# Issuing the first large load ahead of SyncE's part of the entry barrier, in a decode kernel that streams weights and cache

## The chip, the cores and the metric

The kernel runs on one core of one Trainium2 chip. The metric is device microseconds of one execution, in medians of several. The profile's span (first to last instruction) is about 1.25 us shorter than the time of the same run.

## The reference, cut to what matters

One decode step (one token, batch of 2, width 640): adaLN modulation from `c`, attention over the last 1024 positions of a cache with 32 heads of 192, then a gated FFN. At batch 2 nearly all of the work is reading weights and cache once.

```python
x = A_x
mod = (_silu(c) @ w_mod).reshape(c.shape[0], 6, 1, -1)      # w_mod: 640 x 3840
sa, ca, ga, sb, cb, gb = (...)                              # six rows of mod
h = _layernorm(x) * (1 + ca) + sa
x = x + ga * _A_ref(h, A_k_cache, A_v_cache, A_wq, A_wo)    # q = h @ wq, attention, @ wo
h = _layernorm(x) * (1 + cb) + sb
x = x + gb * _B_ref(h, B_w_gate, B_w_up, B_w_down)          # gelu(h@w_gate) * (h@w_up) @ w_down
```

## The kernel before

It moves 77 MB, all large loads by SyncE on one DMA queue, in the order of need: `w_mod`, `wq` (two loads), then K and V tiles through a ring of eight slots, `wo`, and the FFN weights. A small scheduler records every operation with what it reads and writes, works out semaphore waits, and emits one list for each engine at the end. Loads all stand in one line of a helper (L266).

```python
def k_dma(dst, src):
    return lambda e: e.dma_start(dst, src)                   # L266
...
wm_dma = S.dma("sp", k_dma(wm_v..., w_mod...), sem_wm, writes=["wm"], name="ld_wm")
declare_ring()                      # wq (2 loads), K tiles 0 and 1, V tile 0: no wait, the slots are free
S.op("pool", lambda e: e.memset(xr[:, :], 0.0), writes=["xr"], name="xr0")
S.dma("act", k_dma(crow[:, :], c[:, :]), sem_c, writes=["crow"], name="ld_c")
S.dma("act", k_dma(xr[0:P:RB, :], A_x...), sem_x, writes=["xr"], name="ld_x")
... # constants on GpSimd; cT -> SiLU -> scT; x -> statistics; mod = scT @ w_mod -> hT; q = hT @ wq; ...

S.resolve()
S.emit("sp", nc.sync, tail=lambda e: e.wait_ge(sem_out, 16))
S.emit("pool", nc.gpsimd)
S.emit("act", nc.scalar)
S.emit("dve", nc.vector)
S.emit("pe", nc.tensor)
```

Ahead of all of this stands an entry barrier that the program object puts in when it is made (the line of that call, L715, is on its records). GpSimd writes four small constants. Every other engine has a drain (the instruction with which it reports to the barrier) that adds one to a semaphore; GpSimd waits for those four counts, then adds to a second semaphore, and each engine takes its release from that. The barrier keeps any engine from reading the constants before they are written. The load of `w_mod` reads none of them and writes a buffer that nobody has touched yet.

## Time and profile before

| | before |
|---|---|
| time, median (range) of 5 runs | 188.94 us (188.71 to 189.14) |
| span of the profiled run | 187.6 us |
| SyncE's load queue, share of 16 DMA engines' time | 97.1% |
| share of DMA in the chain of waits | 71% |
| first packet of SyncE's queue, from the packet records | 1.81 us |

The page first. The second part cuts the span into 40 slices (the digits are tenths of the slice); the third lists the queues with packets, MB and their share; the fourth is the chain that ended last; the sixth gives KB of one load and the median us from issue to landing.

```profile
DMA  7999998999999999999999999999999999999991
GB/s 254 402 451 435 430 459 372 422 435 424 430 422 422 427 425 426 427 424 420 419 432 432 422 423 422 421 438 422 424 423 422 419 488 428 416 384 442 398 396 45
...
q1 hardware_dynamic: 6492, 76.88, 97.1%
...
DMA 71%; DVE 15%; PE 7%; ACT 2%; SPq 2%; issue 1%
...
ring<-in_A_k_cache_dram SPq DMA_DIRECT2D x16, 1536.0 KB, 24.4
```

The DMA engines have work from the first slice to the last but one. A K tile takes 24.4 us to land, but 1536 KB at about 425 GB/s need only 3.7 us: it waits behind six or seven others. So a K load that is issued a few us sooner or later, because a slot came free sooner or later, should change nothing. Where does a load stream like this leave room? In its start and in what follows its end. These are in the timeline (start us, duration us, engine, line, operation; in brackets, how long the engine had been idle and what ended that) of the first microseconds:

```profile
0.80 0.39 SPq L266 DMA_DIRECT2D r<-in_w_mod_dram  x1
0.81 0.56 ACTq L266 DMA_DIRECT2D crow<-in_c_dram  x1
...
1.25 1.16 SPq L266 DMA_DIRECT2D ring<-in_A_wq_dram  x2
1.30 1.76 DVE L367 MEMSET ps<- 128x2048 f32 x1 [1.30 <-PEq L715]
1.41 0.64 ACTq L266 DMA_DIRECT2D xr<-in_A_x_dram  x1
...
3.43 0.19 ACT L386 ACTIVATE scT<-ps 128x10 bf16<-128x10 bf16 x1
...
9.84 0.24 DVE L388 CAST X<-xr 128x160 f32<-128x160 bf16 x1 [4.33 <-DMA xr<-in_A_x_dram]
...
15.18 2.18 PE L445 MATMUL ps<-r,scT 128*17 128x480 bf16 x20 [3.94 <-DMA r<-in_w_mod_dram]
...
19.58 0.17 DVE L427 CAST hT<-ps 128x10 bf16<-128x10 f32 x1 [0.48 <-PE ps L423]
```

and, from the chain of waits, its second `wq` load, its last K load, the last `w_down` load and the tail:

```profile
1.70 32.29 DMA ring<-in_A_wq_dram
...
120.47 24.62 DMA ring<-in_A_k_cache_dram
...
152.72 31.64 DMA r<-in_B_w_down_dram
...
184.41 0.72 PE ps L684 x16
```

SyncE's own drain and its wait are not in the timeline, which counts work. The records of the trace have them (us from the span's start, duration in ns):

```
0.000    7 SyncE   DRAIN            adds to the first semaphore
0.130   10 VectorE DRAIN            "
0.143    8 ScalarE DRAIN            "
0.316    8 TensorE DRAIN            "
0.304..0.499 GpSimd four constant memsets; its own drain 0.370 to 0.549
0.594   17 GpSimd  waits for four counts
0.672   17 GpSimd  adds to the second semaphore
0.714   17 SyncE   takes its release
0.799  385 SyncE   issues w_mod
1.812      first packet of w_mod
```

SyncE was the first to arrive, at 0.01 us, and then stood for 0.7 us with the whole load stream behind it.

### The profile page before, as it was taken

How to read it: one execution, taken by the hardware profiler on the slowest of the kernel's cores; microseconds unless marked ns; L12 is line 12 of the kernel's file. 1: busy time of each engine (PE TensorE's matmuls, PEld its weight loads, DVE VectorE, ACT ScalarE, POOL GpSimd, SP SyncE). 2: the span in 40 equal slices, each digit the busy share in tenths (PEclk: the TensorE clock that was granted, in tenths of full speed). 3: DMA queues.
4: the chain of work that ended last, by engine and by line, in shares of the span. 5: the costliest groups of instructions: out<-in, count | busy, mean ns of one | idle time of the engine just before them, and what ended most of it. 6: DMA issues, size and time to landing. Idle time of an engine off the chain costs nothing.

```text
span 187.6 us, 2409 instructions
## 1 busy us (share of the span) xinstructions
PE 107.5 (57%) x1039; PEld 51.1 (27%) x1039; DVE 98.2 (52%) x147; ACT 29.9 (16%) x72; POOL 5.1 (3%) x23
## 2 busy tenths in 40 slices
PE   0014730742968887676676655675497395364462
PEld 0011200210323443333423323233253152353121
DVE  6131100019588988886595695775865933003211
ACT  3041100082001221112011110210120103103400
POOL 8200000000000000000000000000000000000000
PEclk9999999997587999999879999999969967569696
DMA  7999998999999999999999999999999999999991
GB/s 254 402 451 435 430 459 372 422 435 424 430 422 422 427 425 426 427 424 420 419 432 432 422 423 422 421 438 422 424 423 422 419 488 428 416 384 442 398 396 45
DMA packets 6518, 77.03 MB, mean 411 GB/s; under 512 B 746, under 2 KB 876, under 8 KB 1516
## 3 DMA queue, kind: packets, MB, share of 16 engines
q1 hardware_dynamic: 6492, 76.88, 97.1%
q8 instruction: 8, 0.13, 0.3%
q10 hardware_dynamic: 16, 0.01, 0.0%
q14 instruction: 2, 0.02, 0.0%
HBM read 76.88 MB, written 0.00 MB: 410 GB/s over the span
## 4 chain that ended last, share of the span: by engine, by line
DMA 71%; DVE 15%; PE 7%; ACT 2%; SPq 2%; issue 1%
DMA ring<-in_A_k_cache_dram 37%; DMA ring<-in_A_wq_dram 17%; DMA r<-in_B_w_down_dram 17%; DVE prod L490 9%; PE ps L502 4%; DVE S_sb L509 4%; PE ps L467 2%; SPq L266 2%; ACT qbc L483 2%; DVE ps L485 1%; DVE M L512 1%; ACT qrow L474 1%; PE ps L526 0%; DVE bcR L519 0%; PE ps L684 0%
## 5 line engine op out<-in xcount | busy, mean ns | idle before, releaser
L490 DVE TENSOR_TENSOR prod<-ring,qbc 128x3072 bf16<-128x3072 bf16 x32 | 55.9, 1751 | 14.3 <-DMA ring<-in_A_k_cache_dram 14.3
L502 PE MATMUL ps<-prod,ident_b 128*128 128x512 bf16 x192 | 52.9, 419 | 14.4 <-DVE prod L490 14.4
L502 PEld LDWEIGHTS ps<-prod,ident_b 128*128 128x128 bf16 x192 | 17.5, 104 | 40.2 <-DVE prod L490 17.5
L509 DVE TENSOR_REDUCE S_sb<-ps 128x32 f32<-128x1024 f32 x16 | 19.3, 1206 | 2.1 <-PE ps L502 2.1
L526 PE MATMUL ps<-bcR,bcL 5*128 5x4 f32 x32 | 6.1, 258 | 21.9 <-DVE bcR L519 21.9
L563 ACT ACTIVATE On<-ps,rden 128x384 bf16<-128x384 f32 x16 | 9.3, 580 | 43.5 <-DVE rden L561 21.1
L551 PE MATMUL ps<-ring,E_sb 128*8 128x384 bf16 x256 | 15.5, 369 | 0.0
L534 ACT ACTIVATE E_sb<-Sb_sb 128x128 bf16<-128x128 f32 x16 | 5.0, 310 | 56.4 <-DVE Sb_sb L531 56.4
L467 PE MATMUL ps<-ring,hT 128*2 128x512 bf16 x60 | 6.7, 626 | 9.8 <-DMA ring<-in_A_wq_dram 8.8
L526 PEld LDWEIGHTS ps<-bcR,bcL 5*128 5x128 f32 x32 | 4.7, 183 | 26.1 <-DVE bcR L519 26.1
L477 DVE CAST qrow<-ps 128x512 bf16<-128x512 f32 x1 | 0.7, 692 | 15.7 <-PE ps L467 15.7
L622 PE MATMUL ps<-ring,oT 128*17 128x160 bf16 x192 | 5.5, 294 | 5.6 <-DMA ring<-in_A_wo_dram 5.6
L531 DVE TENSOR_TENSOR Sb_sb<-S_sb,ps 128x128 f32<-128x128 f32 x16 | 4.6, 287 | 7.6 <-PE ps L526 7.6
L540 PEld LDWEIGHTS ps<-denp,maskc 128*128 128x128 f32 x32 | 7.1, 224 | 3.7 <-ACT E_sb L534 0.9
L641 DVE TENSOR_TENSOR lnt<-ps,modR 128x160 f32<-128x160 f32 x1 | 0.3, 325 | 12.6 <-PE ps L622 12.6
L445 PE MATMUL ps<-r,scT 128*17 128x480 bf16 x40 | 4.3, 597 | 3.9 <-DMA r<-in_w_mod_dram 3.9
L622 PEld LDWEIGHTS ps<-ring,oT 128*17 128x17 bf16 x192 | 4.9, 117 | 6.2 <-DMA ring<-in_A_wo_dram 6.2
L551 PEld LDWEIGHTS ps<-ring,E_sb 128*8 128x8 bf16 x256 | 5.1, 90 | 3.7 <-issue 1.2
L396 PE MATMUL ps<-st,selstat 128*128 128x2 f32 x4 | 0.9, 298 | 8.6 <-ACT sqj L392 8.6
L467 PEld LDWEIGHTS ps<-ring,hT 128*2 128x2 bf16 x60 | 1.7, 114 | 14.7 <-DMA ring<-in_A_wq_dram 9.7
L576 PE MATMUL ps<-On,zsel 128*128 128x96 bf16 x64 | 5.2, 241 | 0.7 <-ACT On L563 0.7
L540 PE MATMUL ps<-denp,maskc 128*128 128x1 f32 x32 | 5.1, 230 | 0.8 <-ACT E_sb L534 0.8
(81 smaller groups left out, 71.2 us busy)
## 6 DMA issues: line engine op xcount, KB each, us to landing
ring<-in_A_k_cache_dram SPq DMA_DIRECT2D x16, 1536.0 KB, 24.4
ring<-in_A_v_cache_dram SPq DMA_DIRECT2D x16, 1536.0 KB, 24.2
r<-in_w_mod_dram SPq DMA_DIRECT2D x1, 4800.0 KB, 14.3
ring<-in_A_wq_dram SPq DMA_DIRECT2D x1, 4608.0 KB, 32.3
ring<-in_A_wo_dram SPq DMA_DIRECT2D x1, 4480.0 KB, 23.4
ring<-in_A_wq_dram SPq DMA_DIRECT2D x1, 3072.0 KB, 21.2
ring<-in_A_wo_dram SPq DMA_DIRECT2D x1, 2720.0 KB, 24.1
r<-in_B_w_gate_dram SPq DMA_DIRECT2D x1, 1920.0 KB, 25.0
```

Source lines behind the costliest of these rows:

```text
L467: last = e.matmul(ps[32 * i:32 * i + B, n, :], lhsT=hT[:, k, :], rhs=wv[:, kk, i, n * QW:(n + 1) * QW], start=(k == 0), stop=(k == KT - 1) ...
L490: S.op("dve", lambda e: e.tensor_tensor(out=prod[:, 2 * (g % 2) + ci, :, :], in0=ring[:, sl, ci * JC * Dh:(ci + 1) * JC * Dh].rearrange("p ...
L502: last = e.matmul(o_ap, lhsT=ident_b[:, :], rhs=prod[:, pz, :, t * GC:(t + 1) * GC], start=(t == 0), stop=(t == NCH - 1))
L509: S.op("dve", lambda e: e.tensor_reduce(out=S_sb[:, z, :], in_=ps[:, 2 * z:2 * z + 2, :].rearrange("p k (j c) -> p (k j) c", c=GC), axis=A ...
L526: S.op("pe", lambda e: e.matmul(ps[:, BK_T, P:P + HQ], lhsT=bcL[:, :], rhs=bcR[:, z, :], start=True, stop=True), reads=[("bcR", z), "bcL"] ...
L531: S.op("dve", lambda e: e.tensor_tensor(out=Sb_sb[:, z, :, :], in0=S_sb[:, z, :].unsqueeze(2).broadcast_to([P, J, HQ]), in1=ps[:, BK_T, P: ...
L534: S.op("act", lambda e: e.activation(out=E_sb[:, z, :, :], in_=Sb_sb[:, z, :, :], func=ACTF.Exp, scale=SCALE, accum_out=denp[:, z:z + 1]), ...
L540: S.op("pe", lambda e: e.matmul(ps[:, BK_T, P + 16:P + 17], lhsT=maskc[:, :], rhs=denp[:, z:z + 1], start=True, stop=True), reads=[("denp" ...
L551: last = e.matmul(ps[32 * i:32 * i + 2 * HQ, BK_O, 0:ON], lhsT=E_sb[:, z, 2 * jp:2 * jp + 2, :].rearrange("p j h -> p (j h)"), rhs=ring[:, ...
L563: S.op("act", lambda e: e.activation(out=On[:, quad % 2, b, :], in_=ps[:, BK_O, 0:ON], func=ACTF.Identity, scale=rden[:, z:z + 1]), reads= ...
L576: last = e.matmul(ps[:, BK_OT, 0:B * NT].rearrange("p (b t) -> p b t", b=B), lhsT=zsel[:, jj, x:x + P], rhs=On[:, quad % 2, :, jj * Dh + d ...
L622: last = e.matmul(ps[32 * i:32 * i + RM, BK_M, 0:DR], lhsT=oT[:, t, :], rhs=wv[:, tl, i, :], start=(t == 0), stop=(t == NT - 1), tile_posi ...
```

## The change: intent and diff

The intent is to start the load stream while the other engines are still coming to the barrier. The instruction that issues `w_mod` is emitted first, cut from the end of the instruction list, and put ahead of SyncE's drain. No other instruction differs.

```diff
         S.resolve()
+        body = nc.main_func.blocks[0].instructions
+        entry = next(i for i, x in enumerate(body) if x.opcode == "Drain" and x.engine == mybir.EngineType.SP)
+        first = S.lists["sp"].pop(0)
+        assert first is wm_dma and not first.waits
+        n0 = len(body)
+        first.fn(nc.sync).then_inc(first.sem, first.inc)
+        moved = body[n0:]
+        del body[n0:]
+        body[entry:entry] = moved
         S.emit("sp", nc.sync, tail=lambda e: e.wait_ge(sem_out, 16))
```

## The prediction

> **What bounds the kernel now.** The load stream. The page's slice rows show the DMA engines 90% or more busy in nearly all slices; the queue part gives SyncE's queue 97.1%. The chain of waits is 71% DMA. K loads take 24.4 us from issue to landing, while 1536 KB at the sustained 425 GB/s need 3.7 us, so six or seven loads are always queued: slot releases by DVE and PE are hidden, and only the stream's start, rate and tail count. The last w_down load lands at 184.4; 16 matmuls, two DVE operations and the store end the span at 187.6.
>
> **What the change does.** No work is removed. In the records of the entry, SyncE drains at 0.00 us (the first instruction of all), waits for the barrier until 0.71, and issues w_mod at 0.80; the issue takes 0.385 us and the first packets start at 1.81, 0.63 us after its end. (The Trainium skill, "DMA: Bandwidth & Descriptors", Specifications, gives about 0.6 us for the first byte on this path; the trace agrees.) After the change the issue begins at 0.00-0.05, packets at about 1.0-1.05. SyncE's arrival at the barrier moves from 0.01 to about 0.45. GpSimd, the collector, takes its step only at 0.59, after its memsets and drain, so SyncE is still not last and the release stays at about 0.7. The first wq load is issued at 0.80 instead of 1.25, long before w_mod's 4.9 MB (12 us) are through, so no gap opens.
>
> **How much is on the critical path.** All of it, about 0.75-0.8 us: the stream starts that much earlier, at once at full rate (254 GB/s in slice one is 414 GB/s after the first packet), and never empties. The computing has slack: hT is ready at 19.75 while the wq loads land at 22.4 and 34.0.
>
> One thing gets worse. c and x go on ScalarE's queue. Now c is issued at 0.81 and its packets start at 1.75, just before w_mod's. Afterwards they find w_mod packets (38 KB, about 2.1 us each) already there. The skill (same page, Queues, rings and completion order) says that each DMA engine alternates between queue rows by whole packets; x's packets (5.4-9.5 us, issued at 1.4) fit that. So c should land at 5-9 us instead of 2.5, and the SiLU move from 3.4 to 6-10. It is needed at w_mod's landing (14.3), so no loss.
>
> **Prediction.** 188.83 - 0.78 = 188.05 us. Range 187.6 to 188.6, from the spread of 0.4 us between runs and different packet interleaving. Faster by over 2%: 0.005; within 2%: 0.985; slower by over 2%: 0.01.
>
> **What would show it.** Timeline: w_mod's issue at 0.0-0.1, wq's at 0.8; barrier release still 0.7; DVE's first memset still 1.3. First packet 1.0-1.1. w_mod landing at 14.3-14.4 instead of 15.1; second wq load 33.2; last w_down load 183.6; span 186.8. c landing late.
>
> **What would make it wrong.**
> - SyncE's drain may wait for the descriptors (harmless, wq is still queued in time) or for the whole load (then c, x and wq start 12 us late and the time grows by several us).
> - An issue that early may start slowly, so that less than 0.78 comes through.
> - c or x may be held until after 13 us and delay the modulation; the slack before wq should absorb some.
> - [...]

## The result, and the profile after

| | before | after |
|---|---|---|
| time, median (range) of 5 runs | 188.94 us (188.71 to 189.14) | 188.08 us (187.95 to 188.16) |
| span of the profiled run | 187.6 us | 186.7 us |
| issue of `w_mod` starts | 0.80 us | 0.00 us |
| first packet | 1.81 us | 1.00 us |
| first packet to last landing of `w_down` | 182.9 us | 182.9 us |
| last landing to the end of the span | 2.9 us | 2.8 us |

The ratio of after to before is 0.9955, with a 95% interval of 0.9943 to 0.9968: 0.85 us. By the bound of 2% that is "the same", but it is clear of noise. A ratio is the mean time of one kernel's runs over the mean of the other's in the same rounds, so it is not quite the ratio of the medians quoted.

The page of the kernel after:

```profile
DMA  8989998999999999999999999999999999999991
GB/s 296 486 366 437 474 422 379 437 427 427 429 424 427 417 426 432 424 424 425 421 427 427 427 430 421 420 429 424 429 422 424 449 462 422 404 402 428 408 399 51
...
q1 hardware_dynamic: 6492, 76.88, 97.6%
...
DMA 72%; DVE 16%; PE 5%; ACT 2%; SPq 1%; issue 1%
...
ring<-in_A_k_cache_dram SPq DMA_DIRECT2D x16, 1536.0 KB, 24.6
```

The timeline of its first microseconds (the barrier's line is L724 here, since the edit added nine lines):

```profile
0.00 0.39 SPq L266 DMA_DIRECT2D r<-in_w_mod_dram  x1
...
0.79 0.81 SPq L266 DMA_DIRECT2D ring<-in_A_wq_dram  x2
0.80 0.55 ACTq L266 DMA_DIRECT2D crow<-in_c_dram  x1
...
1.29 1.76 DVE L367 MEMSET ps<- 128x2048 f32 x1 [1.29 <-PEq L724]
1.40 0.63 ACTq L266 DMA_DIRECT2D xr<-in_A_x_dram  x1
...
8.62 0.19 ACT L386 ACTIVATE scT<-ps 128x10 bf16<-128x10 bf16 x1 [5.27 <-PE ps L383]
12.49 0.24 DVE L388 CAST X<-xr 128x160 f32<-128x160 bf16 x1 [6.98 <-DMA xr<-in_A_x_dram]
...
14.16 2.18 PE L445 MATMUL ps<-r,scT 128*17 128x480 bf16 x20 [0.27 <-DMA r<-in_w_mod_dram]
...
18.56 0.17 DVE L427 CAST hT<-ps 128x10 bf16<-128x10 f32 x1 [0.48 <-PE ps L423]
```

Its chain of waits:

```profile
1.18 31.98 DMA ring<-in_A_wq_dram
...
119.57 24.64 DMA ring<-in_A_k_cache_dram
...
151.85 31.64 DMA r<-in_B_w_down_dram
...
183.93 0.28 PE ps L684 x4
```

Three things are to be seen. First, everything that hangs on the load stream moved forward by about one amount: the first packet by 0.81 us, the second `wq` load from 33.99 to 33.16, the last K load of the chain from 145.09 to 144.21, the last `w_down` load of the chain from 184.37 to 183.50 (a start plus a duration in the chain). Second, the barrier didn't move: VectorE's first memset starts at 1.29, as before. In the records SyncE's drain now stands from 0.450 to 0.561, GpSimd's own drain ends at 0.541, and GpSimd's wait passes at 0.587, as before. That is close: SyncE and GpSimd now reach this step almost together, and "Why the prediction was right" takes this up. Third, `c` and `x`, issued at the same times as before, now land much later: the SiLU starts at 8.62 instead of 3.43, the cast of `x` at 12.49 instead of 9.84. The matmul with `w_mod` still waits for its load and not for them.

### The profile page after: what moved, and what is told of

Read it like the earlier page. It is cut to its first block, busy times and chain, and to the rows that moved or that the text cites. A ratio compares the mean times of both kernels' runs of the same rounds, so it can differ in the third digit from the quotient of the medians.

```text
span 186.7 us, 2408 instructions
## 1 busy us (share of the span) xinstructions
PE 106.9 (57%) x1038; PEld 51.9 (28%) x1039; DVE 98.2 (53%) x147; ACT 30.0 (16%) x72; POOL 5.1 (3%) x23
## 4 chain that ended last, share of the span: by engine, by line
DMA 72%; DVE 16%; PE 5%; ACT 2%; SPq 1%; issue 1%
DMA ring<-in_A_k_cache_dram 38%; DMA ring<-in_A_wq_dram 17%; DMA r<-in_B_w_down_dram 17%; DVE prod L490 10%; DVE S_sb L509 4%; PE ps L502 2%; PE ps L467 2%; ACT qbc L483 2%; SPq L266 1%; DVE ps L485 1%; DVE M L512 1%; ACT qrow L474 1%; DVE bcR L519 0%; PE ps L526 0%; PE ps L684 0%
## 5 line engine op out<-in xcount | busy, mean ns | idle before, releaser
L502 PE MATMUL ps<-prod,ident_b 128*128 128x512 bf16 x192 | 51.5, 411 | 15.7 <-DVE prod L490 15.6
L551 PE MATMUL ps<-ring,E_sb 128*8 128x384 bf16 x256 | 14.8, 356 | 0.0
L622 PE MATMUL ps<-ring,oT 128*17 128x160 bf16 x192 | 6.8, 338 | 5.5 <-DMA ring<-in_A_wo_dram 5.5
L622 PEld LDWEIGHTS ps<-ring,oT 128*17 128x17 bf16 x192 | 6.1, 135 | 6.1 <-DMA ring<-in_A_wo_dram 6.1
L576 PE MATMUL ps<-On,zsel 128*128 128x96 bf16 x64 | 4.6, 223 | 0.7 <-ACT On L563 0.7
L514 PE MATMUL ps<-ident_f,M 128*1 128x128 f32 x16 | 4.5, 280 | 0.4 <-DVE M L512 0.4
## 6 DMA issues: line engine op xcount, KB each, us to landing
r<-in_w_mod_dram SPq DMA_DIRECT2D x1, 4800.0 KB, 14.1
```

The source lines that it names most:

```text
L502: last = e.matmul(o_ap, lhsT=ident_b[:, :], rhs=prod[:, pz, :, t * GC:(t + 1) * GC], start=(t == 0), stop=(t == NCH - 1))
L551: last = e.matmul(ps[32 * i:32 * i + 2 * HQ, BK_O, 0:ON], lhsT=E_sb[:, z, 2 * jp:2 * jp + 2, :].rearrange("p j h -> p (j h)"), rhs=ring[:, ...
L576: last = e.matmul(ps[:, BK_OT, 0:B * NT].rearrange("p (b t) -> p b t", b=B), lhsT=zsel[:, jj, x:x + P], rhs=On[:, quad % 2, :, jj * Dh + d ...
L622: last = e.matmul(ps[32 * i:32 * i + RM, BK_M, 0:DR], lhsT=oT[:, t, :], rhs=wv[:, tl, i, :], start=(t == 0), stop=(t == NT - 1), tile_posi ...
```

## The experiments

The theory, called S in the expectations: only the start of the load stream counts, one to one; what it carries first, who arrives when at the barrier, and when the later loads are issued do not matter as long as the queue never runs empty. The rivals: B, the gain comes from something about the barrier; Q, it comes from the later loads being issued sooner (`wq` at 0.79 instead of 1.25); M, it comes through `w_mod` landing sooner and the modulation. All runs gave correct results and were timed in five rounds. Edits are against the changed kernel unless said otherwise.

### The changed kernel again: after_again, after_third

No edit; a yardstick on two of the three chips used. On the third, that of wq_held, cx_held and the late starts, the changed kernel itself was not run again. Every ratio is to the kernel before in the rounds of its own chip.

> The changed kernel once more, as the yardstick of these four on one chip. All theories: 188.1 us, ratio to before 0.9955 +- 0.001; first packets at 1.00 us, w_mod's landing at 14.1.

> The changed kernel as the yardstick of this chip for the two runs beside it: 188.1 us.

Measured: 188.09 us, ratio to before 0.9959 (0.9947 to 0.9972), and 188.11 us, 0.9951 (0.9938 to 0.9963). The gain repeats.

### Behind the drain, ahead of the wait: behind_drain

```diff
-        body[entry:entry] = moved
+        body[entry + 1:entry + 1] = moved
```

> The issue of w_mod stands behind SyncE's drain and ahead of its wait for the release. Theory S (only the start of the load stream counts): SyncE arrives at the barrier at about 0.01 us as in the kernel before, the issue starts at about 0.05, first packets at about 1.06, time 188.15 us, ratio 0.9955. Rival B (something about SyncE's later arrival, its drain now taking 111 ns, or the shifted barrier gave the gain): the gain goes, 188.9 us.

Measured: 188.22 us (188.13 to 188.44), ratio 0.9968 (0.9955 to 0.9980). From the timeline:

```profile
0.09 0.38 SPq L266 DMA_DIRECT2D r<-in_w_mod_dram  x1
```

SyncE's drain stands at 0.00 again, with 7 ns; the issue starts at 0.085 and the first packet comes at 1.087. Most of the gain stays with the barrier's arrivals as they were in the kernel before, so B falls for the drain and the order of arrival. The 0.13 us over the changed kernel of the same rounds is of the size of the 0.08 us of later first packet; the intervals of the two ratios overlap, so no more can be read from it.

### Another load first: wq_ahead

```diff
-        first = S.lists["sp"].pop(0)
-        assert first is wm_dma and not first.waits
+        first = S.lists["sp"].pop(1)
+        assert first.name.startswith("ld_wq") and not first.waits
```

> The first wq load, not w_mod, is issued ahead of the drain; w_mod is issued first behind the barrier. Theory S: the stream starts at 1.0 us whatever it carries first, so 188.1 us, ratio 0.9955, although w_mod lands at about 21.4 instead of 14.1 and hT is ready at about 26 instead of 18.7 (still ahead of the second wq load, about 33.1). Rival M (the gain came through w_mod's earlier landing and the modulation): w_mod lands 6 us later than in the kernel before, so the time is over that of before by up to 6 us, 189 to 195.

Measured: 188.05 us (188.03 to 188.08), ratio 0.9957 (0.9944 to 0.9969). The timeline:

```profile
0.00 0.39 SPq L266 DMA_DIRECT2D ring<-in_A_wq_dram  x1
...
0.79 0.33 SPq L266 DMA_DIRECT2D r<-in_w_mod_dram  x1
...
25.62 0.17 DVE L427 CAST hT<-ps 128x10 bf16<-128x10 f32 x1 [0.48 <-PE ps L423]
28.35 1.88 PE L467 MATMUL ps<-ring,hT 128*2 128x512 bf16 x16 [0.77 <-ACT modR L450]
```

`w_mod` is issued behind the barrier, at the same 0.79 us as in the kernel before, and lands at 21.2 us, 6 us later than there; `hT` is 7 us later than in the changed kernel. The time is that of the changed kernel. M falls: the gain doesn't depend on which load goes first, and 7 us of delay in the modulation cost nothing.

### Six loads ahead: six_ahead

```diff
-        first = S.lists["sp"].pop(0)
-        assert first is wm_dma and not first.waits
+        early = [S.lists["sp"].pop(0) for _ in range(6)]
+        assert early[0] is wm_dma and not any(o.waits for o in early)
...
-        first.fn(nc.sync).then_inc(first.sem, first.inc)
+        for first in early:
+            first.fn(nc.sync).then_inc(first.sem, first.inc)
```

> All six loads that need no wait are issued ahead of the drain, so SyncE comes to the barrier last, at 3.5 to 4.2 us, and all other engines start some 3 us later. Theory S: the stream's start is the same, so 188.1 us, ratio 0.9955 +- 0.001; x lands at 15 to 16, hT is ready at 20 to 22, still before the second wq load at 33. Rival Q (the gain is SyncE's time: the later loads issued earlier): 0.4 us or more faster than the changed kernel, 187.7. Rival B (the barrier's release time counts): 3 us slower, about 191.

Measured: 188.13 us (187.97 to 188.28), ratio 0.9959 (0.9945 to 0.9972). From the timeline:

```profile
0.00 0.39 SPq L266 DMA_DIRECT2D r<-in_w_mod_dram  x1
0.44 0.89 SPq L266 DMA_DIRECT2D ring<-in_A_wq_dram  x2
1.37 1.28 SPq L266 DMA_DIRECT2D ring<-in_A_k_cache_dram  x2
2.69 0.61 SPq L266 DMA_DIRECT2D ring<-in_A_v_cache_dram  x1
...
3.97 0.56 ACTq L266 DMA_DIRECT2D crow<-in_c_dram  x1
...
19.35 0.17 DVE L427 CAST hT<-ps 128x10 bf16<-128x10 f32 x1 [0.47 <-PE ps L423]
```

Here SyncE is last at the barrier, as `c`'s issue at 3.97 instead of 0.80 shows: all engines start 3.2 us later. The five further early issues gain nothing, and the late barrier costs nothing. Both halves speak for S: `wq` at 0.44 is no better than at 0.79, and three idle microseconds of four engines are hidden behind the stream. (By itself this run can't exclude a gain and a loss that cancel. But wq_ahead and cx_held show that a later modulation costs nothing, and the three runs that follow change the issue times alone.)

### The later loads held back: wq_held, wq_held_again, wq_held_silu

```diff
         S.resolve()
+        held = S.lists["sp"][1]
+        assert held.name.startswith("ld_wq") and not held.waits
+        o = next(o for o in S.lists["pool"] if o.name == "bcRd")
+        held.waits = [(o.sem, o.val)]
```

In wq_held_silu the list is that of ScalarE and the name is `silu`.

> The changed kernel, but SyncE issues the wq loads and all later ones only after GpSimd's last constant (about 6.0 us). Theory S: w_mod's own packets keep the DMA engines busy until about 13, so nothing changes: 188.1 us, ratio 0.9955. Rival Q (part of the gain came from wq's issue moving from 1.25 to 0.80): slower than the changed kernel by at least that 0.45 us, 188.5 or more, up to 193 if issue times count one to one.

> The first hold of the wq loads (about 6.0 us) once more, since it measured 0.26 us above the changed kernel where theory S said 0. Theory S with noise: 188.1, within 0.15 us of the changed kernel. Rival Q in a weak form (late issue costs a little, although the queue is not empty): 188.35 again.

> The hold made longer: SyncE issues wq and all later loads only after the SiLU on ScalarE, at 7.5 to 9 us, still before w_mod's packets are through (about 13). Theory S: 188.1 us, as the changed kernel. Weak rival Q: the cost grows with the hold, 188.5 or more.

The issue of `wq` moved from 0.79 to 6.00, 5.99 and 8.43 us; here that of the first run:

```profile
6.00 0.81 SPq L266 DMA_DIRECT2D ring<-in_A_wq_dram  x2
```

Measured: 188.35 us (188.22 to 188.75), 188.28 (188.14 to 188.80) and 188.24 (188.10 to 188.36); ratios 0.9972 (0.9960 to 0.9985), 0.9966 (0.9951 to 0.9980) and 0.9957 (0.9944 to 0.9969). Q in its full form falls: a delay eleven times as long as the 0.45 us in question costs a third of a microsecond at most, and a longer hold costs no more than a shorter one. The first of the three did miss S's number, by 0.25 us. The changed kernel on the chip of the other two took 188.11 (187.91 to 188.35). Whether a hold costs 0.1 to 0.3 us or nothing is left open. For a small cost: cx_held, a version of the changed kernel in the same rounds as the first hold, took 188.06 to 188.13, all below that hold's lowest run (188.22). Against it: on the chip of the other two the ranges overlap, and the cost does not grow with the hold. The profiled runs show no difference (spans of 186.8 to 186.9 against 186.7 to 186.9), but they were among the faster runs: the two holds to 6 us had spans up to 187.4 and 187.6, the changed kernel up to 187.1. So it is not shown that late issue is free to the last tenth. For the gain in question this matters little: if 0.3 us for a hold of 5.2 us were real and in proportion, `wq`'s 0.45 us would be worth 0.03 us (an estimate).

### The start made later: late_aT0, late_zsel0

These are edits of the kernel before:

```diff
         S.resolve()
+        o = next(o for o in S.lists["pool"] if o.name == "aT0")     # late_zsel0: "zsel0"
+        wm_dma.waits = [(o.sem, o.val)]
```

> The kernel before, with w_mod's issue held until GpSimd's fourth memset is done (2.07 us), so it is issued at about 2.1 instead of 0.80, and all later loads behind it. Theory S: one to one, 1.3 us slower than before, 190.25 us, ratio 1.007. If part of an early start is absorbed later (slack somewhere in the stream), less than 1.0 us comes through.

> The same with a longer hold, until GpSimd's zsel memset (4.71 us): issue at about 4.8, 4.0 us later than before. Theory S: one to one, 192.9 us, ratio 1.021. A hidden slack of the stream would show as a slope below one between this run and the one with the shorter hold (2.7 us between their issues).

Measured: 190.31 us (190.04 to 190.61), ratio 1.0073 (1.0060 to 1.0085), and 193.00 us (192.82 to 193.27), ratio 1.0218 (1.0204 to 1.0232). The timelines, of late_aT0:

```profile
2.08 0.38 SPq L266 DMA_DIRECT2D r<-in_w_mod_dram  x1
```

and of late_zsel0:

```profile
4.75 0.39 SPq L266 DMA_DIRECT2D r<-in_w_mod_dram  x1
...
5.29 0.31 DVE L388 CAST X<-xr 128x160 f32<-128x160 bf16 x1
...
23.40 0.17 DVE L427 CAST hT<-ps 128x10 bf16<-128x10 f32 x1 [0.48 <-PE ps L423]
```

The issue is 1.28 and 3.95 us later than before; the time grew by 1.38 us (0.0073 of 188.95) and 4.12 us (0.0218 of 188.95). One to one, in the direction opposite to the change. Note that `x` is cast at 5.29 in late_zsel0 (and at 5.28 in late_aT0), earlier than in the kernel before (9.84) and the changed one, without any use. Between the two late starts the issue moved by 2.67 us and the time by 2.69: no slack is hidden in the stream.

### c and x held back: cx_held

```diff
         S.resolve()
+        held = next(o for o in S.lists["act"] if o.name == "ld_c")
+        o = next(o for o in S.lists["pool"] if o.name == "bcRd")
+        held.waits = [(o.sem, o.val)]
```

> The changed kernel, but ScalarE issues c and x only after GpSimd's last constant (about 6.0 us instead of 0.8 and 1.4). Theory S: 188.1 us, ratio 0.9955: c lands at 11 to 13 and x at 17 to 18, which delays hT to about 22 to 23 instead of 18.7, still 10 us before the second wq load lands. Rival M (c, x and the modulation are on the critical path, so that their late landing in the changed kernel cost part of the gain): slower by 3 us or more.

Measured: 188.09 us (188.06 to 188.13), ratio 0.9956 (0.9943 to 0.9968). From the timeline:

```profile
6.00 0.55 ACTq L266 DMA_DIRECT2D crow<-in_c_dram  x1
...
14.77 0.24 DVE L388 CAST X<-xr 128x160 f32<-128x160 bf16 x1 [9.27 <-DMA xr<-in_A_x_dram]
20.50 0.17 DVE L427 CAST hT<-ps 128x10 bf16<-128x10 f32 x1 [0.47 <-PE ps L423]
```

`x` came earlier than expected (14.77 instead of 17 to 18), so `hT` was only 1.9 us later than in the changed kernel. That delay cost nothing. The late landing of `c` and `x`, the price of the change, is free here.

### All of them on one line

The first packet is that of SyncE's queue in the profiled run; the stream runs from there to the last landing of `w_down`.

| kernel | first packet, us | stream, us | time, us |
|---|---|---|---|
| before | 1.81 | 182.9 | 188.94 |
| after | 1.00 | 182.9 | 188.08 |
| behind_drain | 1.09 | 183.0 | 188.22 |
| wq_ahead | 1.01 | 182.9 | 188.05 |
| six_ahead | 1.00 | 183.1 | 188.13 |
| wq_held | 1.01 | 183.0 | 188.35 |
| cx_held | 1.01 | 182.8 | 188.09 |
| late_aT0 | 3.09 | 183.1 | 190.31 |
| late_zsel0 | 5.76 | 183.0 | 193.00 |

The stream has one length in all of them, within 0.3 us. The packet records show no moment, in any of these runs, in which SyncE's queue had no packet under way, from its first packet to its last packet of `w_down`, which ends 0.4 us before the last landing. No experiment pointed to a version that beats the changed kernel: further early issues and another order left the time where it was, and the stream's length was not touched.

## Why the prediction was right

- **The size.** It forecast 188.05 us; 188.08 was measured. The argument was one sum, 188.83 minus the distance by which the first packets move, 0.78; they moved by 0.81 and the time fell by 0.85. That the forecast hit within 0.03 us is partly luck: the base of 188.83 was the median of the three runs known then, 0.11 us below that of all five, and the gain was forecast 0.08 us too small (0.86 between the medians), so two small errors cancelled. The later starts and the changed one give slopes of 1.04 to 1.08 us per us (1.38 over 1.28, 4.12 over 3.95, 0.85 over 0.81), which within the intervals are one.
- **All on the critical path.** Shown by the two late starts, which paid in full, and by the constant stream.
- **The barrier.** "SyncE is still not last" held only as a tie. The drain took 111 ns behind the issue, where 7 ns were read before, so SyncE arrived at 0.56 and not at 0.45. In six_ahead, where SyncE is surely last, GpSimd's step comes 25 ns after the end of SyncE's drain; in the kernel before it comes 45 ns after the end of GpSimd's own. In the changed kernel it comes 26 ns after the one and 46 ns after the other, so there is no margin left, and in wq_ahead (26 and 53 ns) SyncE was last by some 7 ns. The release stayed at 0.71 all the same, as forecast. Nothing hung on it, as six_ahead showed with an arrival 3 us later.
- **The drain doesn't wait for the load.** This was the largest risk named. Behind one issue it ended at 0.56 us, behind six at 3.73, while `w_mod` landed at 14.1 in both.
- **What gets worse.** `c` was expected at 5 to 9 us and landed at 8.18; the SiLU was expected at 6 to 10 and started at 8.62. The Trainium skill ("DMA: Bandwidth & Descriptors", Queues, rings and completion order) says that an engine alternates between queue rows by whole packets. This agrees with the trace, where `c` had packets at 1.75 us when it came before `w_mod` and at 4.6 and 6.3 us when it came after. The runs show the delay and not the arbitration itself. The prediction gave no number for `x`, whose cast moved from 9.84 to 12.49. It was the tighter of the two: what is computed from it was ready at 14.96 and used at 17.70, 2.7 us later, while the SiLU was done 5.4 us before the matmul that needs it. In the two repeats the SiLU started at 6.94 and 7.04 and the cast at 10.82 and 10.89, so the delay differs from run to run.
- **Slack of the modulation.** It was said to be free, and is: `hT` at 19.4, 20.5 and 25.6 us cost nothing in six_ahead, cx_held and wq_ahead.
- **A detail off.** `w_mod`'s landing was put at 14.3 to 14.4; it came at 14.12, and at 14.25 and 14.29 in the repeats. In the kernel before, its last DMA engine was 0.48 us behind the one before it (14.66 and 15.14), in the profiled run after 0.24 (13.88 and 14.12). Why was not examined, and it has no part in the gain, since the second `wq` load moved by 0.83.

## What to carry to other kernels

Where a profile shows one load queue busy from its first packet to the tail, the time is the first packet plus the length of the stream plus the tail, so look at what stands ahead of the first issue. In this kernel a start 0.8 us sooner was worth 0.8 us, and issuing the second and later loads sooner still brought nothing that could be measured. A load that depends on nothing the entry barrier protects can stand ahead of it; check that it writes a buffer nobody else uses yet and that its own semaphore guards its readers. Then ask who is pushed back: small loads on another queue now meet a full stream, here 3 to 6 us later (1 to 4 in the repeats), which was free only because the first user of the result waited for a large load anyway.

## What the Trainium skill lacked or had wrong

- "DMA: Bandwidth & Descriptors", Specifications: the row names about 358 GB/s as the limit of HBM for one core and does not say that this is a share with both cores of a pair reading. The same page says so further down (Bandwidth), with 425 GB/s measured on one core alone. This kernel, on one core, read HBM at 410 GB/s over its whole span and at 425 GB/s between 40 and 145 us, so the row by itself would mislead here.
- The same page, Specifications, gives about 0.6 us to the first byte on SyncE's path. That agrees if it is counted from the end of the issue (0.61 to 0.64 us over these runs); from the start of the issue it was 1.00 to 1.01 us, and the page doesn't say which is meant.
- No page that we read says what SyncE's drain does with loads under way: it took 7 ns with none, 111 ns behind one issue and 372 ns behind six, and did not wait for their landing (14 us for the first).
- No page that we read gives the cost of a kernel's own entry barrier: here 0.71 us from the first drain to the release, set by GpSimd's constants and its drain.
